# A chunked delta rule with routed experts: stacked keys in the front, block-diagonal copies by ScalarE, half blocks in 64x64 tiles, readerless products

## The chip, the core and the metric

The kernel runs on one core of a Trainium2 chip. Five engines run their own instruction streams: TensorE (PE, with its weight loads shown as PEld), VectorE (DVE), ScalarE (ACT), GpSimd (POOL) and SyncE (SP, which here only issues DMA transfers). They wait for each other by semaphores. The metric is the device time of one execution in microseconds. The profile comes from one execution of its own.

## The reference, cut to what matters

Two blocks follow each other. The first is a delta rule with B=4 batches, H=8 heads, 768 time steps and head size D=48; the second sends each of the 3072 resulting rows (384 wide) to one of eight experts.

```python
k_n = k / (np.linalg.norm(k, axis=-1, keepdims=True) + 1e-06)
state = np.zeros((B, H, D, D), dtype=np.float32)
for t in range(S):
    kt, vt, bt = (k_n[:, :, t], v[:, :, t], beta[:, :, t, None])
    y[:, :, t] = np.einsum('bhd,bhde->bhe', q[:, :, t], state)
    v_old = np.einsum('bhde,bhd->bhe', state, kt)
    state = state + bt[:, :, :, None] * np.einsum('bhd,bhe->bhde', kt, vt - v_old)
# ...  x = y as (3072, 384)
logits = x @ w_gate
expert_idx = np.argmax(logits, axis=1)
# ...  gate_w: the softmax of the chosen logit; rows sorted by expert
    h = np.maximum(x_sorted[lo:hi] @ w1[e], 0.0)
    y_sorted[lo:hi] = h @ w2[e]
# ...
return (gate_w[:, None] * y).astype(np.float32)
```

## The kernel before

Time is cut into 24 steps of C=32 tokens. The 128 partitions hold the 32 tokens of each of the four batches. For a step, PE forms the scores (keys by keys, keys by queries) of all heads; DVE masks them into `km`; DVE inverts the 32x32 triangular blocks of four steps (a group) at once, a long chain of small operations (`invert`). A step then takes the state's answer to its keys (`pv`, copied out as R), multiplies it by the inverted block (`pz`, copied out as Z), and adds keys by Z to the state (`acc`, copied out as `states`). Rows of the output go to DRAM (`xs`), their logits decide the expert, and after the last step the experts run over gathered rows.

Keys and queries lie in DRAM as `kq_t[step, 96, 4, 2, 128]`: two heads stacked on 96 partitions, four pairs, key or query, four batches of 32 tokens. A product over 96 partitions mixes the two heads of a pair, unless one operand is block-diagonal: `wide_kq` holds, for each of the two heads, a copy that is zero in the other's rows.

The program does not leave the order to a scheduler: instructions stand on each engine in the order in which these lines run.

How keys are loaded and scores formed:

```python
    def load_plain(c, k):

        t = kq_buffer()[0:D].rearrange("d p k t -> d (p k) t")
        for e, eng in enumerate((nc.sync, nc.scalar)):
            eng.dma_start(out=t[:, NP * e : NP * e + NP, :], in_=kq_t[c, D * e : D * e + D, :, k, :])
        return t

    def load_kq(c):
        if c < NS:
            if c not in kqs:
                kqs[c] = kq_buffer()
            nc.sync.dma_start(out=kqs[c][:], in_=kq_t[c])

    def load_wide(c):
        if c < NS:
            for e in range(2):
                r = slice(D * e, D * e + D)
                nc.sync.dma_start(out=wide_kq[c % 3][r, e], in_=kq_t[c, r])

    def plain_scores(pa, keys, others):

        for h in range(H):
            for b in range(B):
                j = NP * (h % 2) + h // 2
                nc.tensor.matmul(
                    pa[rows_of(b), C * h : C * h + C], lhsT=keys[:, j, rows_of(b)],
                    rhs=others[:, j, rows_of(b)], start=True, stop=True, skip_group_check=True,
                )

    def front_scores(c, pa):

        wide = wide_kq[c % 3]
        for p in range(NP):
            for b in range(B):
                for e in range(2):
                    nc.tensor.matmul(
                        pa[rows_of(b), 128 * p + 64 * e : 128 * p + 64 * e + 64],
                        lhsT=wide[:, e, p, 0, rows_of(b)], rhs=wide[:, e, p, :, rows_of(b)],
                        start=True, stop=True, skip_group_check=True,
                    )
        load_wide(c + 3)
        return c, pa

    def scores(c):

        if c >= NS:
            return None
        wide, kq = wide_kq[c % 3], kqs[c]
        pa = psA.tile([128, 512], FP32, name="pa", tag="pa")
        for p in range(NP):
            for b in range(B):
                nc.tensor.matmul(
                    pa[rows_of(b), 128 * p : 128 * p + 128], lhsT=kq[:, p, 0, rows_of(b)],
                    rhs=wide[:, :, p, :, rows_of(b)], start=True, stop=True,
                    skip_group_check=True,
                )
        load_wide(c + 3)
        return pa
```

The first group of steps (0 to 3) is inverted in halves of 16 tokens; two products by half blocks (`across`) then complete each of its steps. Copies by ACT with `own` as scale lay a block into two columns, one of them zero, so that two batches share a 64x64 tile:

```python
    def across(gt, fdt, ub, s):

        W = C // 2
        part = ub[:, H * s : H * s + H, W:C]
        m1 = work.tile([128, H, W], FP32, name="m1")

        def product(l, r):
            po = psA.tile([128, 512], FP32, name="pa", tag="pa")
            for h in range(H):
                for b in range(B):
                    nc.tensor.matmul(
                        po[rows_of(b), W * h : W * h + W], lhsT=l[rows_of(b), H * s + h],
                        rhs=r[rows_of(b), h], start=True, stop=True, skip_group_check=True,
                    )
            return po[:, 0 : H * W]

        po = product(gt, part)
        nc.scalar.activation(out=m1[:].rearrange("p h w -> p (h w)"), in_=po, func=AF.Copy)

        def second():
            po = product(fdt, m1)
            chores.appendleft(partial(added, po))

        def added(po):
            nc.vector.tensor_tensor(
                out=part, in0=part, in1=po.rearrange("p (h w) -> p h w", h=H), op=OP.add
            )

        chores.appendleft(second)

    def chore():
        if chores:
            chores.popleft()()

    def spread_out(steps=(0, GS)):

        g, ub = spread[0]
        if g not in ubs:
            ubs[g] = block.tile([128, GS * H, 2, C], FP32, name="ubw")
        a, b = (H * s for s in steps)
        for k in range(2):
            nc.scalar.activation(
                out=ubs[g][:, a:b, k], in_=ub[:, a:b], func=AF.Copy, scale=own[:, k : k + 1]
            )
        if steps[1] == GS:
            spread.popleft()
```

Products of the identity with itself, which nothing reads, keep TensorE at work, and `fill` gives DVE a budget of inversion work:

```python
    def heat(n=1, out=None):

        if out is None:
            out = psA.tile([128, 512], FP32, name="pa", tag="pa")[:]
        for _ in range(n):
            nc.tensor.matmul(
                out, lhsT=ident[:],
                rhs=ident[:].unsqueeze(1).to_broadcast([128, out.shape[1] // 128, 128]),
                start=True, stop=True, skip_group_check=True,
            )
```

A step, and the front and the loop around it:

```python
        if c == 0:
            R = vs
        else:
            by_state(pv, 0, False)
            R = work.tile([128, H, D], FP32, name="R")
            nc.scalar.activation(
                out=R[:].rearrange("q h w -> q (h w)"), in_=pv[:, 0:DM], func=AF.Copy
            )
            if c < LATE:
                ranked()
                logits()
        if c >= LATE:
            turn(c - 1)
        scale_v(c + 1, 0)
        for h in range(H):
            for r in two_of:
                nc.tensor.matmul(
                    pz[r, D * h : D * h + D],
                    lhsT=ub[r, H * s + h].rearrange("q k w -> q (k w)"),
                    rhs=R[r, h, :], start=(h == 0), stop=True, skip_group_check=True,
        chore()
        Z = work.tile([128, H, D], FP32, name="Z")
        # ... Z <- pz by ScalarE
        if c > 0:
            by_state(pq, 1, True)
        # ...
        load_kq(c + LEAD + 1)
        if c < GS:
            load_kq(c + GS)
        extra = score() if c in EXTRA else None
        scale_v(c + 1, 1)
        # ... acc += keys by Z; load_kt(c + 2); states <- acc; chore(); pq += km by Z
        nc.scalar.activation(out=x, in_=pq[:, 0:DM], func=AF.Copy, scale=-1.0)
        nc.sync.dma_start(out=xs[128 * c : 128 * c + 128, 0:DM], in_=x)
        if spread and GS <= c and c >= GS * (spread[0][0] - 1):
            spread_out()
        return extra

    # ... the front
    keys = [load_plain(c, 0) for c in range(GS)]
    nc.scalar.dma_start(out=cf[:, 0:CS], in_=src[:, 0:CS])
    nc.scalar.dma_start(out=beta[:], in_=beta_blk)
    for i in (1, 2, 0):
        t = wide_kq[i][:].rearrange("q e p k w -> q (e p k w)")
        for j, eng in enumerate(((nc.vector, nc.gpsimd), (nc.gpsimd, nc.vector))[i % 2]):
            eng.memset(t[:, 1024 * j : 1024 * j + 1024], 0.0)
    for c in range(GS, GS + 3):
        load_wide(c)
    queries = [load_plain(c, 1) for c in range(GS)]
    nc.gpsimd.memset(states[:], 0.0)
    nc.gpsimd.memset(empty[:], FAR)
    first = {c: ss for ss in BATCHES for c in ss}
    load_vt(0)
    load_kt(0)
    for c in range(1, LEAD + 1):
        kqs[c] = kq_buffer()
    load_kq(1)

    kms[0] = km_buffer()
    for c in range(GS):
        pool, name = ((psA, "pa"), (psQ, "pq"), (psC, "pv"), (psC, "pz"))[c]
        pa = pool.tile([128, 512], FP32, name=name, tag=name)
        plain_scores(pa, keys[c], keys[c])
        keep_plain(c, 0, pa[:, 0 : H * C], mask_0)
    behind.append([0, invert(0), 0.0])
    ahead = [front_scores(GS, acc[:, 2, :]), front_scores(GS + 1, acc[:, 3, :])]
    load_vt(1)
    load_kt(1)
    for c in range(GS):
        a = H * C * (c % 2)
        plain_scores(acc[:, c // 2, a : a + H * C], keys[c], queries[c])
    load_kq(2)
    ahead.append(front_scores(GS + 2, psC.tile([128, 512], FP32, name="pv", tag="pv")))
    load_kq(8)
    ahead.append(front_scores(GS + 3, psQ.tile([128, 512], FP32, name="pq", tag="pq")))
    load_kq(9)
    load_kq(3)
    heat(3)
    while not spread:
        fill(0.1)
    scale_v(0, 0)
    scale_v(0, 1)
    begin(0)
    chore()
    keep_plain(0, 1, acc[:, 0, :], mask[:, C : 2 * C])
    keep_scores(*ahead[0])
    chore()
    keep_scores(*ahead[1])
    chore()
    spread_out((0, 1))
    # ...
    for c in range(NS):
        # ...
        if c % GS == 0 and c // GS not in ubs:
            while not spread:
                fill(0.1)
            spread_out()
        extra = step(c)
        fill(4.0)
        # ...
        if c < GS - 1:
            chore()
            spread_out((c + 1, c + 2))
        # ...
        more = score()
        if c + 1 < NS:
            begin(c + 1)
        fill(3.2)
        keep_scores(*more)
        if c == GS:
            weights[0] = start_w(wpool)
            pieces.extend(pieces_w(moe_w1[0], moe_w2[0], *weights[0]))
        if pieces:
            pieces.popleft()()
```

Of the kernel before, what the change touches and what calls it, by code (L numbers as in the profile page):

```python
# [22 lines left out]
DD = 2 * D  # L23
# [8 lines left out]
E = 8  # L32
# [21 lines left out]
def _f32_consts():  # L54

    p = np.arange(128)[:, None]
    j = np.arange(128)[None, :]
    rev = np.broadcast_to(E - np.arange(E), (128, E))
    base = np.broadcast_to(np.arange(E) * LIST, (128, E))
    more = np.arange(E)[:, None] * LIST + CAP + np.arange(MAXR)[None, :] * 128
    more = np.broadcast_to(more.reshape(1, -1), (128, E * MAXR))
    t, w = p % C, j[:, :C]
    kk = 1.0 * (t == w) - (t < w)
    own = 1.0 * (p // C % 2 == np.arange(2)[None, :])
    half = t // (C // 2) == w // (C // 2)  # L70
    k0 = 1.0 * (t == w) - ((t < w) & half) - (t // (C // 2) > w // (C // 2))
    kq = -1.0 * (t < w)
    mine = -1.0 * (p // D == np.arange(2)[None, :])
    return np.concatenate(
        [kk, kq, k0, own, mine, rev, base, more, p < j, np.ones((128, 128))], axis=1
    ).astype(np.float32)
# [3 lines left out]
def kernel(  # L80
# [23 lines left out]
    CS = 3 * C + 4  # L104
# [3 lines left out]
    def part(w):  # L108
# [4 lines left out]
    mask, mask_0, own, mine, rev, base, further, upper, ones = (  # L113
        part(w) for w in (2 * C, C, 2, 2, E, E, E * MAXR, 128, 128)
# [164 lines left out]
    scored, front, now = [0], [None], [0]  # L279
# [34 lines left out]
    def load_plain(c, k):  # L314

        t = kq_buffer()[0:D].rearrange("d p k t -> d (p k) t")
        for e, eng in enumerate((nc.sync, nc.scalar)):
            eng.dma_start(out=t[:, NP * e : NP * e + NP, :], in_=kq_t[c, D * e : D * e + D, :, k, :])
        return t
# [6 lines left out]

    def load_wide(c):
        if c < NS:
            for e in range(2):
                r = slice(D * e, D * e + D)  # L330
                nc.sync.dma_start(out=wide_kq[c % 3][r, e], in_=kq_t[c, r])
# [11 lines left out]
    def plain_scores(pa, keys, others):  # L343

        for h in range(H):
            for b in range(B):
                j = NP * (h % 2) + h // 2
                nc.tensor.matmul(
                    pa[rows_of(b), C * h : C * h + C], lhsT=keys[:, j, rows_of(b)],
                    rhs=others[:, j, rows_of(b)], start=True, stop=True, skip_group_check=True,  # L350
                )

    def front_scores(c, pa):

        wide = wide_kq[c % 3]
        for p in range(NP):
            for b in range(B):
                for e in range(2):
                    nc.tensor.matmul(
                        pa[rows_of(b), 128 * p + 64 * e : 128 * p + 64 * e + 64],  # L360
                        lhsT=wide[:, e, p, 0, rows_of(b)], rhs=wide[:, e, p, :, rows_of(b)],
                        start=True, stop=True, skip_group_check=True,
                    )
        load_wide(c + 3)
        return c, pa

    def scores(c):
# [3 lines left out]
        wide, kq = wide_kq[c % 3], kqs[c]  # L371
        pa = psA.tile([128, 512], FP32, name="pa", tag="pa")
# [7 lines left out]
        load_wide(c + 3)  # L380
# [136 lines left out]
    def across(gt, fdt, ub, s):  # L517
# [3 lines left out]
        m1 = work.tile([128, H, W], FP32, name="m1")  # L521

        def product(l, r):
            po = psA.tile([128, 512], FP32, name="pa", tag="pa")
            for h in range(H):
                for b in range(B):
                    nc.tensor.matmul(
                        po[rows_of(b), W * h : W * h + W], lhsT=l[rows_of(b), H * s + h],
                        rhs=r[rows_of(b), h], start=True, stop=True, skip_group_check=True,
                    )  # L530
            return po[:, 0 : H * W]

        po = product(gt, part)
        nc.scalar.activation(out=m1[:].rearrange("p h w -> p (h w)"), in_=po, func=AF.Copy)

        def second():
            po = product(fdt, m1)
# [13 lines left out]
    def spread_out(steps=(0, GS)):  # L551

        g, ub = spread[0]
        if g not in ubs:
            ubs[g] = block.tile([128, GS * H, 2, C], FP32, name="ubw")
        a, b = (H * s for s in steps)
        for k in range(2):
            nc.scalar.activation(
                out=ubs[g][:, a:b, k], in_=ub[:, a:b], func=AF.Copy, scale=own[:, k : k + 1]
            )  # L560
        if steps[1] == GS:
            spread.popleft()
# [38 lines left out]
    def step(c):  # L601
        g, s = divmod(c, GS)
        kq, ub, kt, vs, km = kqs.pop(c, None), ubs[g], kts.pop(c), vss.pop(c), kms[g]
# [13 lines left out]
        else:  # L617
# [5 lines left out]
            if c < LATE:  # L623
                ranked()
                logits()
        if c >= LATE:
# [15 lines left out]
        if c > 0:  # L642
            by_state(pq, 1, True)
        if c >= LATE:
# [3 lines left out]
        if c == NS - 1:  # L648
            ahead_of_time(1)
        load_kq(c + LEAD + 1)  # L650
        if c < GS:
            load_kq(c + GS)
        extra = score() if c in EXTRA else None
        scale_v(c + 1, 1)
        if c < NS - 1:
# [10 lines left out]
            for e in range(2):  # L666
                nc.scalar.activation(  # L667
                    out=states[:, :, :, e], func=AF.Copy, scale=mine[0:DD, e : e + 1],
# [15 lines left out]
        if c == ss[0]:  # L684
            n = len(ss)
            xgs[c] = work.tile([128, n, ROW], FP32, name=f"xg{n}", bufs=3 if n == 1 else 2)
# [4 lines left out]
        if spread and GS <= c and c >= GS * (spread[0][0] - 1):  # L691
            spread_out()
        return extra

    def score():
        c = scored[0]
        scored[0] += 1
        return c, scores(c)
# [133 lines left out]
    keys = [load_plain(c, 0) for c in range(GS)]  # L832
    nc.scalar.dma_start(out=cf[:, 0:CS], in_=src[:, 0:CS])
    nc.scalar.dma_start(out=beta[:], in_=beta_blk)
    for i in (1, 2, 0):
        t = wide_kq[i][:].rearrange("q e p k w -> q (e p k w)")
        for j, eng in enumerate(((nc.vector, nc.gpsimd), (nc.gpsimd, nc.vector))[i % 2]):
            eng.memset(t[:, 1024 * j : 1024 * j + 1024], 0.0)
    for c in range(GS, GS + 3):
        load_wide(c)  # L840
    queries = [load_plain(c, 1) for c in range(GS)]
# [3 lines left out]
    load_vt(0)  # L845
    load_kt(0)
    for c in range(1, LEAD + 1):
        kqs[c] = kq_buffer()
    load_kq(1)

    kms[0] = km_buffer()
    for c in range(GS):
        pool, name = ((psA, "pa"), (psQ, "pq"), (psC, "pv"), (psC, "pz"))[c]
        pa = pool.tile([128, 512], FP32, name=name, tag=name)
        plain_scores(pa, keys[c], keys[c])
        keep_plain(c, 0, pa[:, 0 : H * C], mask_0)
    behind.append([0, invert(0), 0.0])
    ahead = [front_scores(GS, acc[:, 2, :]), front_scores(GS + 1, acc[:, 3, :])]
    load_vt(1)
    load_kt(1)  # L860
    for c in range(GS):
        a = H * C * (c % 2)
        plain_scores(acc[:, c // 2, a : a + H * C], keys[c], queries[c])
    load_kq(2)
    ahead.append(front_scores(GS + 2, psC.tile([128, 512], FP32, name="pv", tag="pv")))
    load_kq(8)
    ahead.append(front_scores(GS + 3, psQ.tile([128, 512], FP32, name="pq", tag="pq")))
    load_kq(9)
    load_kq(3)
    heat(3)  # L870
# [5 lines left out]
    chore()  # L876
    keep_plain(0, 1, acc[:, 0, :], mask[:, C : 2 * C])
# [4 lines left out]
    spread_out((0, 1))  # L882
# [12 lines left out]
    for c in range(NS):  # L895
# [3 lines left out]
        if c % GS == 0 and c // GS not in ubs:  # L899
            while not spread:  # L900
                fill(0.1)
            spread_out()
        extra = step(c)
        fill(4.0)
        if extra:
            keep_scores(*extra)
        if c < GS - 1:
            chore()
            spread_out((c + 1, c + 2))
# [9 lines left out]
        fill(3.2)  # L919
        keep_scores(*more)  # L920
        if c == GS:
# [193 lines left out]
```

## Time and profile before

| what | value |
|---|---|
| time, three runs | 635.75 us median (631.23 to 637.58) |
| span of the profiled execution | 630.8 us |
| recurrence with its front / experts | 309.0 us / 321.8 us |
| PE busy | 560.4 us (89%), 7660 products |
| PEld busy | 371.1 us (59%), 7661 loads |
| DVE busy | 249.0 us (39%), 818 instructions |
| ACT busy | 184.2 us (29%), 474 instructions |
| POOL busy | 105.1 us (17%), 111 instructions |
| moved by DMA | 68.97 MB |

A busy share over the whole span says little here, since the two parts have different limits; the profile is read by stages. In a row of the timeline, the first number is the start and the second the time from the first instruction of the group to the end of its last, in microseconds; in brackets stands the idle time of the engine ahead of it and what ended it. "issue" means that nothing which the profile shows ended the wait. In a row of waits stand the engine and line that waited, what it waited for, the sum in microseconds, how many times, and the longest. The clock is the share of TensorE's full clock that was granted.

### The profile page before, as it was taken

How to read it: one execution, taken by the hardware profiler on the slowest of the kernel's cores; microseconds unless marked ns; L12 is line 12 of the kernel's file. 1: busy time of each engine (PE TensorE's matmuls, PEld its weight loads, DVE VectorE, ACT ScalarE, POOL GpSimd, SP SyncE). 2: the span in 40 equal slices, each digit the busy share in tenths (PEclk: the TensorE clock that was granted, in tenths of full speed). 3: DMA queues.
4: the chain of work that ended last, by engine and by line, in shares of the span. 5: the costliest groups of instructions: out<-in, count | busy, mean ns of one | idle time of the engine just before them, and what ended most of it. 6: DMA issues, size and time to landing. Idle time of an engine off the chain costs nothing. (4 is left out here: it accounts for less than half of the span.)

```text
span 630.8 us, 17552 instructions
## 1 busy us (share of the span) xinstructions
PE 560.4 (89%) x7660; PEld 371.1 (59%) x7661; DVE 249.0 (39%) x818; ACT 184.2 (29%) x474; POOL 105.1 (17%) x111
## 2 busy tenths in 40 slices
PE   4378888879889899788999999999999999999990
PEld 4356666767767677566867555555555555455550
DVE  4845567997999979311410201111011110201100
ACT  0214536565465665563201101011011110111100
POOL 3000000010110202121137004014140231401011
PEclk9997758897888987685799999999999999999996
DMA  9857535676584322221017634223343223400000
GB/s 167 171 129 211 130 106 133 187 157 176 155 156 116 92 80 64 40 66 40 14 28 278 223 111 146 86 74 131 124 151 103 83 94 125 150 8 32 1 23 14
DMA packets 41632, 68.97 MB, mean 109 GB/s; under 512 B 10758, under 2 KB 31670, under 8 KB 41552
## 3 DMA queue, kind: packets, MB, share of 16 engines
q1 hardware_dynamic: 34128, 57.05, 33.4%
q0 software_dynamic: 4640, 9.47, 4.7%
q10 hardware_dynamic: 2784, 1.29, 1.2%
q8 instruction: 61, 1.00, 0.7%
q14 instruction: 19, 0.16, 0.1%
HBM read 59.02 MB, written 10.35 MB: 110 GB/s over the span
## 5 line engine op out<-in xcount | busy, mean ns | idle before, releaser
L993 PE MATMUL phe<-xTe,w1t 128*128 128x448 f32 (+1 forms) x384 | 136.2, 515 | 0.0
L1009 PE MATMUL pye<-w2t,hT 128*128 128x384 f32 x352 | 114.8, 486 | 0.0
L993 PEld LDWEIGHTS phe<-xTe,w1t 128*128 128x128 f32 x384 | 71.0, 190 | 60.4 <-issue 58.5
L1009 PEld LDWEIGHTS pye<-w2t,hT 128*128 128x128 f32 x352 | 66.9, 190 | 47.1 <-issue 2.6
L809 POOL DMA_INDIRECT lists<-ids,ri x24 | 24.0, 1001 | 277.8 <-DVE tmp L492 142.5
L998 DVE TENSOR_SCALAR hT<-phe 128x448 f32<-128x448 f32 (+1 forms) x32 | 18.9, 592 | 116.4 <-PE phe L993 104.3
L497 DVE TENSOR_TENSOR ut<-ut,tmp 128x58 f32<-128x58 f32 (+9 forms) x164 | 53.1, 324 | 5.4
L492 DVE TENSOR_TENSOR tmp<-ut 128x58 f32<-128x58 f32 (+9 forms) x164 | 52.8, 322 | 5.2
L180 POOL DMA_INDIRECT out_dram<-y,rows x22 | 21.9, 997 | 183.4 <-ACT y L1018 154.1
L571 ACT ACTIVATE vs<-vt,normt 128x48 f32<-128x48 f32 x192 | 47.9, 325 | 1.8 <-issue 1.8
L1002 ACT ACTIVATE hT<-phe 128x448 f32<-128x448 f32 (+1 forms) x32 | 16.6, 517 | 105.7 <-PE phe L993 105.7
L667 ACT ACTIVATE states<-acc,cf 96x768 f32<-96x768 f32 x46 | 38.7, 891 | 21.8 <-PE acc L659 19.4
L1018 ACT ACTIVATE y<-pye,xin 128x384 f32<-128x384 f32 x15 | 8.7, 581 | 122.5 <-PE pye L1009 122.5
L631 PE MATMUL pz<-R,ubw 64*64 64x48 f32 x736 | 29.9, 237 | 14.5 <-ACT lg L733 8.0
L988 DVE COPY xTe<-px 128x448 f32<-128x448 f32 (+1 forms) x24 | 13.3, 580 | 66.5 <-PE px L984 55.9
L631 PEld LDWEIGHTS pz<-R,ubw 64*64 64x64 f32 x736 | 26.8, 151 | 18.0 <-ACT lg L733 9.2
L678 PE MATMUL pq<-Z,km 32*32 32x48 f32 x1536 | 31.7, 230 | 6.3 <-issue 6.1
L678 PEld LDWEIGHTS pq<-Z,km 32*32 32x32 f32 x1536 | 25.5, 125 | 13.0 <-issue 12.6
L659 PE MATMUL acc<-Z,kt 32*96 32x96 f32 x736 | 29.1, 311 | 2.8 <-issue 1.5
L1014 DVE TENSOR_SCALAR y<-pye,xin 128x384 f32<-128x384 f32 x7 | 4.3, 618 | 68.3 <-PE pye L1009 68.3
L609 PEld LDWEIGHTS pv<-states,kq 96*32 96x32 f32 x736 | 17.4, 121 | 18.8 <-issue 11.7
L659 PEld LDWEIGHTS acc<-Z,kt 32*96 32x96 f32 x736 | 24.4, 210 | 6.4 <-issue 3.6
(142 smaller groups left out, 641.3 us busy)
## 6 DMA issues: line engine op xcount, KB each, us to landing
w1t<-in_moe_w_dram SPq DMA_DIRECT2D x7, 1536.0 KB, 12.3
w2t<-in_moe_w_dram SPq DMA_DIRECT2D x7, 1536.0 KB
kq<-in_kq_t_dram SPq DMA_DIRECT2D x23, 384.0 KB, 6.2
wkq<-in_kq_t_dram SPq DMA_DIRECT2D x40, 192.0 KB, 4.0
vt<-in_v_tok_dram SPq DMA_DIRECT2D x24, 192.0 KB, 2.9
kt<-in_k_tok_dram SPq DMA_DIRECT2D x24, 192.0 KB, 4.3
xs<-xg SPq DMA_DIRECT2D x24, 192.0 KB, 7.1
w1t<-in_moe_w_dram SPq DMA_DIRECT2D x6, 256.0 KB
```

Of the source, the lines that this page charges most:

```text
L180: nc.gpsimd.indirect_dma_start(out=out, out_offset=bass.IndirectOffsetOnAxis(ap=index, axis=0), in_=y[0:w, :], in_offset=None, bounds_chec ...
L492: nc.vector.tensor_tensor(out=tv, in0=ud[:, :, j + 1 : W, j].unsqueeze(3).to_broadcast([128, K, n, j]), in1=ud[:, :, j, 0:j].unsqueeze(2). ...
L497: nc.vector.tensor_tensor(out=ud[:, :, j + 1 : W, 0:j], in0=ud[:, :, j + 1 : W, 0:j], in1=tv, op=OP.add)
L571: nc.scalar.activation(out=vss[c][:, h, :], in_=vts[c][:, h, :], func=AF.Copy, scale=norms[g][:, H * s + h : H * s + h + 1],)
L631: nc.tensor.matmul(pz[r, D * h : D * h + D], lhsT=ub[r, H * s + h].rearrange("q k w -> q (k w)"), rhs=R[r, h, :], start=(h == 0), stop=Tru ...
L659: nc.tensor.matmul(acc[0:DD, b, DD * p : DD * p + DD], lhsT=kt[rows_of(b), 2 * p : 2 * p + 2, :], rhs=Z[rows_of(b), 2 * p : 2 * p + 2, :], ...
L667: nc.scalar.activation(out=states[:, :, :, e], func=AF.Copy, scale=mine[0:DD, e : e + 1], in_=acc[0:DD, :, 0:DM].rearrange("q b (p e w) -> ...
L678: nc.tensor.matmul(pq[rows_of(b), D * h : D * h + D], lhsT=km[rows_of(b), H * s + h, 1], rhs=Z[rows_of(b), h, :], start=(c == 0 and h == 0 ...
L809: nc.gpsimd.indirect_dma_start(out=lists, out_offset=bass.IndirectOffsetOnAxis(ap=ri[:, i : i + 1], axis=0), in_=ids[:, ss[i] : ss[i] + 1] ...
L993: nc.tensor.matmul(ph[:], lhsT=w1t[:, s, f * 128 : f * 128 + 128], rhs=xT[:, s, :], start=(s == 0), stop=(s == NK - 1),)
L998: nc.vector.tensor_scalar(out=hT[:, f, :], in0=ph[:], scalar1=0.0, scalar2=None, op0=OP.max)
L1009: nc.tensor.matmul(py[:], lhsT=hT[:, f, t * 128 : t * 128 + w], rhs=w2t[:, f, :], start=(f == 0), stop=(f == NF - 1),)
```

## The change

Four things are changed, and the instructions' order with them.

- **Stacked keys.** Steps 0 to 3 no longer load the 48 rows of each head by themselves and multiply head by head; they load stacked halves (keys first, queries later) and use a block-diagonal copy, so that one product serves a pair of heads.
- **Block-diagonal copies by ScalarE up to step 7.** The copies for steps 0 to 7 are made on the chip from the stacked tile, by an activation with a 0/1 scale per partition (four of them by DVE), and not loaded by two DMA transfers each into zeroed tiles. For later steps they are loaded as before, and those of steps 8 to 10 follow the front's other loads.
- **Half blocks in 64x64 tiles.** The products of `across` take two batches at once, with block-diagonal copies of the left factor, made by ScalarE for step 0 and by GpSimd for steps 1 to 3.
- **Readerless products.** A 128x256 product into `pz` precedes the block product of steps 1 to 15; some of 128x512 stand in the front, in step 0 and, once no scores are left to form, at the end of each step.

Besides, the blocks are spread step by step and not group by group, DVE's budget is 8.6 us and not 7.2 per step up to step 9, and the first expert's weights begin to load at step 9 and not 4.

```diff
-    def load_plain(c, k):
-        t = kq_buffer()[0:D].rearrange("d p k t -> d (p k) t")
-        for e, eng in enumerate((nc.sync, nc.scalar)):
-            eng.dma_start(out=t[:, NP * e : NP * e + NP, :], in_=kq_t[c, D * e : D * e + D, :, k, :])
-        return t
+    def load_half(c, k, eng):
+        if c not in kqs:
+            kqs[c] = kq_buffer()
+        eng.dma_start(out=kqs[c][:, :, k, :], in_=kq_t[c, :, :, k, :])
...
+    def widen(c):
+        for e in range(2):
+            nc.scalar.activation(
+                out=wide_of(c)[:, e], in_=kqs[c][:], func=AF.Copy, scale=this[0:DD, e : e + 1]
+            )
...
+    def widen_half(c, k, w, i):
+        for e in range(2):
+            out, in_ = w[:, e, :, i, :], kqs[c][:, :, k, :]
+            if e or k:
+                nc.scalar.activation(out=out, in_=in_, func=AF.Copy, scale=this[0:DD, e : e + 1])
+            else:
+                nc.vector.tensor_scalar(
+                    out=out, in0=in_, scalar1=this[0:DD, 0:1], scalar2=None, op0=OP.mult
+                )
...
+    def half_scores(c, pa, w, i):
+        for p in range(NP):
+            for b in range(B):
+                nc.tensor.matmul(
+                    pa[rows_of(b), 64 * p : 64 * p + 64], lhsT=kqs[c][:, p, 0, rows_of(b)],
+                    rhs=w[:, :, p, i, rows_of(b)], start=True, stop=True, skip_group_check=True,
+                )
...  # across
+        l1, l2 = (both(t[:, H * s : H * s + H], pool=s > 0) for t in (gt, fdt))
-                for b in range(B):
+                for q in two_of:
                     nc.tensor.matmul(
-                        po[rows_of(b), W * h : W * h + W], lhsT=l[rows_of(b), H * s + h],
-                        rhs=r[rows_of(b), h], start=True, stop=True, skip_group_check=True,
+                        po[q, W * h : W * h + W], lhsT=l[q, h].rearrange("q k w -> q (k w)"),
+                        rhs=r[q, h], start=True, stop=True, skip_group_check=True,
                     )
...  # step
             if c < LATE:
                 ranked()
                 logits()
+                heat(1, pz[:, 0:256])
...
+        else:
+            heat(1, pq[:])
...
-        if c < GS:
-            load_kq(c + GS)
...
-        if spread and GS <= c and c >= GS * (spread[0][0] - 1):
-            spread_out()
+        if c >= GS - 1:
+            spread_out(c + 1)
...  # score
+        if c >= NS:
+            heat()
...  # the front
+    for c in range(GS):
+        load_half(c, 0, (nc.sync, nc.scalar)[c % 2])
...
+    for c in range(GS, 2 * GS):
+        load_kq(c)
+    load_vt(0)
+    load_kt(0)
+    for c in range(GS):
+        load_half(c, 1, nc.sync)
+    for c in range(2 * GS, LEAD + 1):
+        load_kq(c)
+        load_vt(c - 2 * GS + 1)
+        load_kt(c - 2 * GS + 1)
...
+    for c in range(FRONT, FRONT + 3):
+        load_wide(c)
-    heat(3)
+    heat(4)
...
     chore()
+    heat(1, front[0][1][:])
...
     chore()
-    spread_out((0, 1))
+    heat(1, front[0][1][:])
+    spread_out(0)
...  # the loop
-        fill(4.0)
+        fill(4.0 if c > LEAD else 4.6)
...
-        fill(3.2)
+        fill(3.2 if c > LEAD else 4.0)
...
-        if c == GS:
+        if c == LEAD:
             weights[0] = start_w(wpool)
```

## The prediction

> **What bounds the kernel now.** I read the forty slices first: the first 309 us hold the recurrence and the last 321 us the experts, where PE is at 9 tenths and the granted clock at full rate. The change touches nothing in the second part, so I take its 321 us as fixed. I then cut the first part at the starts of the 24 evictions of `pz` (the ACT rows for Z, one per step; Z0 at 46.56, Z4 at 101.46, Z20 at 261.98 us) and asked for the busy time in each stage. The columns are PE, PEld, DVE, ACT, POOL, clock, DMA share, GB/s.
>
> ```profile
> 0.00:46.56 46.56, 25.03 (x998) 20.02 (x999) 26.71 (x77) 5.47 (x18) 5.81 (x13) 0.99 0.78 156
> 46.56:59.45 12.89, 10.91 (x340) 8.58 (x343) 9.26 (x38) 5.91 (x17) 0.00 (x0) 0.62 0.88 246
> 73.83:89.79 15.96, 12.16 (x299) 9.25 (x295) 9.70 (x30) 6.28 (x18) 0.00 (x0) 0.70 0.36 104
> 121.28:132.16 10.88, 9.53 (x240) 7.50 (x244) 9.85 (x37) 5.39 (x15) 2.10 (x2) 0.85 0.36 93
> 230.11:238.04 7.93, 7.27 (x219) 5.78 (x215) 7.11 (x32) 5.64 (x19) 0.97 (x1) 1.00 0.29 79
> 282.26:296.16 13.90, 12.04 (x211) 8.95 (x212) 1.87 (x14) 5.00 (x14) 3.69 (x4) 0.60 0.16 46
> ```
>
> Four regimes show. The front (46.56 us) has no engine busy for even 60% of it. Steps 0 to 3 last 54.9 us at a mean clock near 0.7. Steps 4 to 19 last 160.5 us with DVE busy for 134.2 us, the sum of those stages: DVE, which inverts the blocks, is the bound there. The last steps have an idle DVE and a step of 7.9 us at clock 1.00 but 13.9 us at 0.60.
>
> For the front I read the weight loads in order of time and who waited.
>
> ```profile
> 11.80 0.55 PEld L348 LDWEIGHTS pz<-kq 48*32 48x32 f32 x33 [2.24 <-issue]
> 12.41 2.89 PEld L359 LDWEIGHTS acc<-wkq 96*32 96x32 f32 x93
> 18.30 1.14 PEld L359 LDWEIGHTS acc<-wkq 96*32 96x32 f32 x35 [3.00 <-issue]
> 19.61 1.36 PEld L348 LDWEIGHTS acc<-kq 48*32 48x32 f32 x93 [0.17 <-issue]
> 24.77 1.80 PEld L348 LDWEIGHTS acc<-kq 48*32 48x32 f32 x128 [3.80 <-issue]
> 30.97 0.61 PEld L348 LDWEIGHTS acc<-kq 48*32 48x32 f32 x35 [4.40 <-issue]
> ```
>
> The loads between two "issue" waits are 33+93, 35+93 and 128: always about 128, each with a product beside it, so 256 instructions. The page's queues give the cause:
>
> ```profile
> q8 instruction: 61, 1.00, 0.7%
> ```
>
> 61 packets of 16.4 KB carry about 15,300 PE instructions, one packet per 256. PE is waiting for its own program, 13.4 us in these four waits, while data fill the DMA engines. What this delays is in the timeline:
>
> ```profile
> 30.00 1.02 DVE L509 STREAM_TRANSPOSE fdt<-ut 128x512 f32<-128x512 f32 x1
> 36.08 4.39 PE L584 MATMUL pa<-ident 128*128 128x512 f32 x6
> 40.53 0.73 PE L527 MATMUL pa<-ub,km 32*32 32x16 f32 x64
> ```
>
> DVE has the first inverse at 31.0; the product that reads it starts at 40.53, as PE still had scores and three readerless products in front of it.
>
> For the steps I read the waits, of DVE over 44 to 102 us and of PE over 102 to 222 us:
>
> ```profile
> DVE ub L541 <- PE pa L527: 10.9, 3, 5.0
> DVE km L399 <- PE pa L375: 6.9, 4, 4.4
> ```
> ```profile
> PE pz L631 <- ACT lg L733: 5.3, 11, 1.6
> ```
>
> In steps 0 to 3 DVE, which will be the bound later, loses 17.8 us waiting for PE: whatever makes PE earlier there hands DVE an earlier start on all its inversions. The third line is the gap that the new 128x256 product meets.
>
> [...] the same 32 score loads and products take 1.94 us at 52.10 and 1.08 us at 126.81. [...] 32 products in 64x64 tiles (57.37) take 1.14 us but 64 in 32x32 tiles (58.43) take 0.73 us: halving the count of half-block products saves program, not array time.
>
> **The change, part by part.**
>
> *Front program.* By the order of instructions the matmuls up to step 1's opening one fall from 595 to 343. Each is four instructions here (16 matmuls show as 32 loads and 32 products), so 252*4/256 = 3.9 blocks less: three of the four long waits should go. The stacked-key product of a step takes 32 records instead of 64.
>
> *Front data.* Keys for steps 0 to 3 (0.79 MB), whole kq for 4 to 7 (1.57), v and k of step 0 (0.39), queries (0.79), constants (0.15) must land before PE ends the front: 3.7 MB. Before moved 6.97 MB in 45 us at a mean 155 GB/s, about 190 while busy, so the last query lands near 22 us.
>
> *ScalarE copies.* 128x1024 takes 1.1 us (two in 2.19 us), 128x256 0.45 and 96x768 0.85. Eight 96x1024 copies at 1.1 and twelve 96x512 ones at about 0.6 (four more go to DVE) make 16 us, in step with the landings and done near 24. PE then has about 25 us, and heat(4), 8 records at 4.39/6 = 0.73 us, ends at 31. DVE's chain took 18.0 us from the last masked key (12.95); the memsets go, the stacked keys need a copy first, so it starts near 12 and ends near 30. The block product starts at 31 to 34 instead of 40.5: **-8 us**. The two readerless products after it fill waits of 0.4 and 1.3 us with about 1.6 us: +0.5.
>
> *Steps 0 to 3.* 31 matmuls less in each of steps 1 and 2: half a block each, -1 us with the 1.1 to 2.4 us per "issue" wait found there. Array time of six 64x64 half-block products +0.4 each, +2. The wide keys of step 8 are now queued behind a load that waits for step 0's state product, so step 0's scores wait some 2 us. Spreading one step (0.9 us) instead of four (2.19) ahead of step 4: -1.3. Better clock from the readerless products: PE is busy for 44.5 us at about 0.72; at 0.85 it is 38, -6. Sum: **-4 us**.
>
> *Steps 4 to 19.* The 128x256 product waits, in the order of instructions, for ACT's lg, and so does the block product: R is already there. So it doesn't fill that wait but follows it, 2 records at some 0.2 us at full clock, +0.4 us on PE's chain in each of 14 steps. DVE is the bound there, so most of that hides. Its larger budget up to step 9 (8.6 us instead of 7.2 per step) and fewer half-clock stages let DVE go from 84% to perhaps 87%: 134.2/0.87 = 154, **-6 us**.
>
> *Steps 20 to the end of the recurrence.* 47 us at clocks 0.60, 1.00, 0.60, 0.50. Steps at 1.00 take 8.7. A 128x512 product per step from step 15 costs up to 0.85 us where nothing else waits, and if it keeps half the slow stages warm: **-4 us** net.
>
> Sum: -8 + 0.5 - 4 - 6 - 4 = -21.5 us, 635.75 to **614 us**.
>
> **The rivals.** (1) *Data, not program, holds the front.* [...] if the queries land near 30 rather than 22, the front gains 3 us instead of 8. The DMA share of 0.9 over the first 28 us speaks for it, the 3 MB less to move before the product against. It gives 619 us. (2) *The readerless product is pure cost.* If the clock doesn't change, 14*0.4 and 9*0.6 add 11 us and the clock gains (6 + 4 + some of 6) go: 628 us. For it: it stands behind lg, in no wait of its own. Against: stages at full clock are 2 to 6 us shorter than the slow ones. (3) *The clock stays full throughout.* Steps 20 to 24 at 8.7 to 10 us and DVE at 92% give another 12 us: 602 us.
>
> **Range and chances.** Rival 3 sets the low end, 602; between rivals 1 and 2 lies the high end, 626. A gain of over 2% means under 623.0 us; only rival 2, or rival 1 with half of the clock gain gone, misses that. Faster 0.78, within 2% 0.19, slower 0.03.
>
> **What would show it.** Right: "issue" waits of under 4 us in sum ahead of the first block product; that product at 31 to 34 us; Z4 near 90, Z20 near 245; about 56 packets on the instruction queue; clock of the stages after Z4 nearer to 0.95. Wrong: PE waiting for DMA or ACT's copies past 28 us in the front; step 0's scores waiting over 3 us for the wide keys; the wait of the block product for lg replaced by the readerless product with clocks still at 0.6 to 0.8; experts of other than 321 us.

## The result, and the profile after

The changed kernel takes 615.55 us in the median of four runs (606.83 to 620.98), against 636.66 us of the kernel before on the same chip. The ratio is 0.9588, with a 95% interval of 0.9464 to 0.9712: faster.

The profile comes from an execution of 617.1 us, a slow one for this kernel. A second profile of the same kernel (run e5, below) has 608.6 us; where the two differ, both are given. First the queue that carries PE's program, from the page's list of queues (packets, MB, share):

```profile
q8 instruction: 56, 0.92, 0.7%
```

Five packets less, as counted. Next the stages between the Z evictions, with the same columns as before (PE, PEld, DVE, ACT, POOL busy; clock; DMA share; GB/s):

```profile
0.00:41.13 41.13, 27.49 (x525) 20.02 (x527) 27.24 (x86) 23.15 (x43) 8.79 (x17) 0.92 0.53 134
41.13:60.04 18.91, 16.50 (x274) 12.20 (x277) 10.19 (x36) 5.90 (x17) 3.75 (x5) 0.50 0.61 158
74.43:84.17 9.74, 9.29 (x271) 7.25 (x266) 7.27 (x25) 6.28 (x18) 0.00 (x0) 1.00 0.51 145
121.77:132.43 10.66, 9.51 (x241) 7.32 (x242) 10.03 (x34) 6.17 (x17) 2.02 (x2) 0.91 0.65 141
220.30:230.75 10.45, 8.18 (x215) 6.14 (x211) 9.28 (x36) 6.33 (x20) 0.97 (x1) 1.00 0.50 105
271.10:282.46 11.36, 9.54 (x215) 7.26 (x215) 1.87 (x14) 5.67 (x16) 3.69 (x4) 0.85 0.36 87
```

The front has half the records of before on PE (525 for 998) and four times the work on ACT. Step 2 (third row) fell from 15.96 to 9.74 us at full clock; step 0 (second row) grew from 12.89 to 18.91 at half clock. Rows 4 and 5 belong to the stretch that the prediction has bound by DVE. Row 4 is step 7, which took 10.44 us in the kernel before (the prediction's row at 121.28 us is step 6). Row 5 is step 17 both times and takes 10.45 us for 7.93 at the same full clock, with DVE busy for 9.28 us and not 7.11.

The sums by stretch, where an expert's first `phe` product ends the last one:

| stretch | before | after | after again (e5) |
|---|---|---|---|
| front, to Z0 | 46.6 us | 41.1 us | 38.3 us |
| steps 0 to 3, Z0 to Z4 | 54.9 us | 51.6 us | 44.4 us |
| steps 4 to 19, Z4 to Z20 | 160.5 us | 159.9 us | 161.3 us |
| Z20 to the first expert product | 68.4 us | 63.8 us | 64.1 us |
| from there to the end | 300.4 us | 300.7 us | 300.5 us |

PE's weight loads in the front show what took the place of the waits for program:

```profile
8.33 0.87 PEld L368 LDWEIGHTS pv<-wkq,kq 96*32 96x32 f32 x32 [1.19 <-issue]
13.04 0.84 PEld L368 LDWEIGHTS pz<-wkq,kq 96*32 96x32 f32 x32 [3.85 <-ACT wkq L348]
15.12 1.48 PEld L382 LDWEIGHTS acc<-wkq,kq 96*32 96x32 f32 x32 [1.24 <-ACT wkq L329]
17.20 1.48 PEld L382 LDWEIGHTS acc<-wkq,kq 96*32 96x32 f32 x32 [0.60 <-ACT wkq L329]
26.26 0.49 PEld L368 LDWEIGHTS acc<-wkq,kq 96*32 96x32 f32 x32 [0.73 <-ACT wkq L348]
```

Of the four long "issue" waits of before one of 1.19 us is left; PE now waits for ScalarE's copies, 0.6 to 1.2 us a time, and once 3.85 us for the keys of step 3. The first block product starts at 32.01 us where it was 40.53.

### The profile page after: what moved, and what is told of

Read it like the earlier page. It is cut to its first block, busy times and chain, and to the rows that moved or that the text cites. A ratio compares the mean times of both kernels' runs of the same rounds, so it can differ in the third digit from the quotient of the medians.

```text
span 617.1 us, 16442 instructions
## 1 busy us (share of the span) xinstructions
PE 568.3 (92%) x7076; PEld 370.3 (60%) x7077; DVE 248.4 (40%) x820; ACT 207.1 (34%) x529; POOL 113.3 (18%) x120
## 5 line engine op out<-in xcount | busy, mean ns | idle before, releaser
L1041 DVE TENSOR_SCALAR hT<-phe 128x448 f32<-128x448 f32 (+1 forms) x32 | 18.9, 591 | 116.4 <-PE phe L1036 96.2
L692 ACT ACTIVATE states<-acc,cf 96x768 f32<-96x768 f32 x46 | 38.7, 891 | 16.4 <-PE acc L684 15.3
L1031 DVE COPY xTe<-px 128x448 f32<-128x448 f32 (+1 forms) x24 | 13.3, 580 | 66.5 <-PE px L1027 55.9
L656 PE MATMUL pz<-R,ubw 64*64 64x48 f32 x736 | 28.5, 231 | 4.5 <-ACT R L644 4.1
L703 PE MATMUL pq<-Z,km 32*32 32x48 f32 x1536 | 27.7, 228 | 2.7 <-issue 2.7
L684 PE MATMUL acc<-Z,kt 32*96 32x96 f32 x736 | 27.6, 294 | 1.0 <-issue 1.0
L703 PEld LDWEIGHTS pq<-Z,km 32*32 32x32 f32 x1536 | 23.5, 124 | 7.1 <-issue 6.7
L684 PEld LDWEIGHTS acc<-Z,kt 32*96 32x96 f32 x736 | 22.9, 195 | 5.6 <-issue 2.1
L203 POOL DMA_INDIRECT xin<-xs,rows x22 | 22.4, 1019 | 10.7 <-DMA rowh<-lists 4.6
```

The lines of the kernel that those rows point to most:

```text
L203: nc.gpsimd.indirect_dma_start(out=xin[0:w, t, :], out_offset=None, in_=xs, in_offset=bass.IndirectOffsetOnAxis(ap=index, axis=0), bounds_ ...
L656: nc.tensor.matmul(pz[r, D * h : D * h + D], lhsT=ub[r, H * s + h].rearrange("q k w -> q (k w)"), rhs=R[r, h, :], start=(h == 0), stop=Tru ...
L684: nc.tensor.matmul(acc[0:DD, b, DD * p : DD * p + DD], lhsT=kt[rows_of(b), 2 * p : 2 * p + 2, :], rhs=Z[rows_of(b), 2 * p : 2 * p + 2, :], ...
L692: nc.scalar.activation(out=states[:, :, :, e], func=AF.Copy, scale=minus[0:DD, e : e + 1], in_=acc[0:DD, :, 0:DM].rearrange("q b (p e w) - ...
L703: nc.tensor.matmul(pq[rows_of(b), D * h : D * h + D], lhsT=km[rows_of(b), H * s + h, 1], rhs=Z[rows_of(b), h, :], start=(c == 0 and h == 0 ...
```

## The experiments

Each run below is timed against the kernel before on the same chip, in three series on three chips (e1 to e4, e5 to e8, e9 to e12; the changed kernel itself ran only in the second); ratios carry their 95% interval. A stage time comes from the one profile of its run, and the clock scatters from profile to profile (Z0 to Z1 of the changed kernel: 0.50 and 0.78), so differences of stages under some 2 us are not read.

**e5: the changed kernel again.** No edit.

> The changed kernel once more, as the reference for the others of this series on the same chip. Both theories expect a ratio to before of 0.955 to 0.970. If the 18.9 us from Z0 to Z1 in its first profile came from the wait for the wide keys of step 8 alone, they come again; if half of it was the phase in which the clock fell, this profile shows 14 to 16 us as the three other variants with the same front did, and the wait for the wide keys (2.4 us) again.

612.04 us in the median against 633.8 (602.67 to 623.15, too scattered for an interval). Z0 to Z1 was 15.3 us, with a 3.9 us wait of the scores for the wide keys. So about 3.5 us of the 18.9 came with the half clock that the first profile has from 34.9 us on, before Z0. That didn't come again, and what set it off isn't shown; the wait for the keys came again.

**e1: no early v and k of step 2.**

```diff
         load_kq(c)
-        load_vt(c - 2 * GS + 1)
-        load_kt(c - 2 * GS + 1)
+        if c == 2 * GS:
+            load_vt(1)
+            load_kt(1)
```

> The front no longer loads v and k of step 2; nothing else is changed. Theory (the wide keys of step 8 were queued behind a load that waits for step 0's state product, so step 0's scores waited 2.4 us for them [...]): the start of the score product of step 0 comes within 0.5 us of the end of the output products before it, Z0 to Z1 falls from 18.9 us to 14 to 16, ratio to before 0.945 to 0.955. Rival (step 0 is slow because the clock is at half rate anyway from 35 us on[...]): the wait goes but Z0 to Z1 stays over 17.5 us, ratio 0.957 to 0.962.

606.62 us against 631.96, ratio 0.9624 (0.9549 to 0.9699). In PE's timeline of the changed kernel, step 0's scores stand behind a wait (named after DVE, which had long been done; what they wait for is the landing of `wkq`, which SyncE issued at 44.9 us, after the `kt` load that needed step 0's `acc`):

```profile
46.21 1.50 PE L703 MATMUL pq<-Z,km 32*32 32x48 f32 x64
50.12 1.93 PE L382 MATMUL pa<-wkq,kq 96*32 96x128 f32 x32 [2.41 <-DVE tmp L500]
```

In e1 they follow at once and at full clock, and the step takes half of what it took:

```profile
40.73 1.01 PE L703 MATMUL pq<-Z,km 32*32 32x48 f32 x64
41.67 1.08 PE L382 MATMUL pa<-wkq,kq 96*32 96x128 f32 x32
```
```profile
38.06:47.53 9.47, 9.45 (x278) 7.11 (x281) 8.54 (x35) 5.90 (x17) 3.74 (x5) 1.00 0.39 112
```

Z0 to Z1 is 9.5 us here, in e6 and in e9, which all lack the early loads; e2, e3, e4, e5, e10 and e11, which have them, show 14.8 to 15.6 at clocks of 0.77 and 0.78, and the first profile 18.9. The theory holds for the wait, and its size was too small: 5 to 6 us, since a lower clock went with the wait (the scores behind it take 1.94 us in e2 and e5, 1.08 in e1). The ratio is another matter: 0.9624 lies in the rival's range and not in the theory's. Z4 comes at 76.7 us (80.4 to 85.8 in e2, e3 and e4 on the same chip), but Z20 at 242.5 (241.0 to 246.3 there): what step 0 gained is gone by then.

**e2: the fourth step's keys first.**

```diff
-        load_half(c, 0, (nc.sync, nc.scalar)[c % 2])
+        load_half(c, 0, nc.scalar if c == 1 else nc.sync)
```

> The fourth step's keys are issued on SyncE's queue ahead of the whole tiles of steps 4 to 7, and not on ScalarE's beside them. Theory (in the changed kernel DVE's chain began at 14.6 us and not at 12 because these keys shared the DMA engines with later data and landed at 12.3): the last masked keys are done by 11.5 us, the chain ends 3 us earlier, and the first block product follows it by as much only if PE's program and readerless products are done by then: 29 to 30 us and not 32.0; ratio 0.950 to 0.955. Rival (ScalarE's 16 us of copies and the data behind them hold PE): the chain ends earlier but the block product stays at 31.5 or later, ratio 0.957 to 0.961.

609.98 us against 631.96, ratio 0.9649 (0.9516 to 0.9782): no gain over the changed kernel can be told by time. By profile the mechanism is there. DVE's last masked keys and the first transposition of its chain, in the changed kernel and in e2:

```profile
14.19 0.42 DVE L396 TENSOR_TENSOR km<-pz,cf 128x256 f32<-128x256 f32 x1 [1.11 <-PE pz L368]
14.65 2.17 DVE L429 STREAM_TRANSPOSE ut<-km 128x256 f32<-128x256 f32 x4
```
```profile
9.83 0.42 DVE L396 TENSOR_TENSOR km<-pz,cf 128x256 f32<-128x256 f32 x1 [0.43 <-PE pz L368]
10.29 2.15 DVE L429 STREAM_TRANSPOSE ut<-km 128x256 f32<-128x256 f32 x4
```

The chain starts 4.4 us earlier and the block product at 28.7 us instead of 32.0, now right behind the readerless products, which end at 28.6. Z4 comes at 80.4 us, but Z20 at 246.3.

**e6: both changes of order.** The edits of e1 and e2 together.

> Both changes of order: step 2's v and k no longer loaded in the front, the fourth step's keys ahead of later data. If the two gains add: first block product at 27 to 29 us, Z0 near 34, Z1 near 44, Z4 near 73, and a ratio 0.01 below the changed kernel's of the same series. Rival (DVE's inversions bound everything up to step 20, so what the front gives is taken back): Z4 as early, but Z20 still at 241 to 246 us as in the four variants so far, and the ratio within 0.005 of the changed kernel's.

605.69 us against 633.8, ratio 0.9572 (0.9528 to 0.9615). The block product came at 30.7 us, behind the four readerless products of the front, which ended at 30.6; Z1 at 46.9, Z4 at 75.8 us and not 73. Z20 came at 234.1 us. It is earlier than in the other profiles, so the rival's fixed Z20 falls, but Z4 to Z20 is 158.3 us, as ever. Against the changed kernel's median of the same series the gain is 1%, and the scatter of that kernel's runs is larger.

**e3: no 128x256 products.**

```diff
                 ranked()
                 logits()
-                heat(1, pz[:, 0:256])
```

> The 128x256 product ahead of the block product in steps 1 to 15 is left out. Theory of the prediction (it costs 0.4 to 0.6 us a step on PE, mostly hidden behind DVE, and buys clock): the mean clock from Z1 to Z15 falls by 0.05 or more, and the time from Z1 to Z15 grows by 2 to 5 us; ratio 0.962 to 0.968. Rival (pure cost): the clock stays within 0.03 and Z1 to Z15 shrinks by 5 to 8 us; ratio 0.946 to 0.951. Third (DVE hides cost and gain alike): within 2 us either way.

610.29 us against 631.96, ratio 0.9724 (0.9632 to 0.9815). Mixed: the clock from Z1 to Z15 stayed (0.92, with the products 0.92 and 0.94), Z1 to Z15 shrank to 136.0 us from 143.2 and 140.0, but the time did not. No theory holds whole; e9 takes it up.

**e4: no late 128x512 products.**

```diff
         scored[0] += 1
-        if c >= NS:
-            heat()
         return c, scores(c)
```

> The 128x512 product at the end of steps 15 to 23 is left out. Theory (it keeps the clock up where PE has no scores to form, and that is worth more than its 0.85 us): the mean clock from Z16 to the end of the recurrence falls from about 0.89 to 0.75 or less and this stretch grows by 3 to 6 us; ratio 0.963 to 0.968. Rival (pure cost): the clock stays within 0.03, the stretch shrinks by 4 to 6 us; ratio 0.949 to 0.953.

610.31 us against 631.96, ratio 0.9668 (0.9574 to 0.9761). The clock from Z16 to the first expert product fell to 0.82 (0.87 and 0.85 with them), and the stretch took 103.4 us (104.8 and 105.4 with them). Both theories miss, each by its other half: the clock fell, but no change of time that could be read came of it. Within the stretch, Z20 to the first expert product is 66.4 us, longer than in any other profile of the changed kernel and its variants (55.9 to 64.1), and Z16 to Z20 is shorter (37.0 us, with the products 41.0 and 41.3).

**e7: the readerless products alone, in the kernel before.**

```diff
                 logits()
+                heat(1, pz[:, 0:256])
...
         scored[0] += 1
+        if c >= NS:
+            heat()
```

> The kernel before, with the 128x256 product ahead of the block product in steps 1 to 15 and the 128x512 one at the end of steps 15 to 23, and nothing else of the change. Theory of the prediction (they bring 5 to 8 us by the clock): mean clock from Z1 to Z15 over 0.88 (0.84 without), ratio 0.985 to 0.992. Rival (they cost what they bring, and the whole gain is the front's and the first steps'): ratio 0.995 to 1.01, Z1 to Z15 within 3 us of 153.

638.42 us against 633.8, ratio 1.0071 (1.0007 to 1.0135). The theory's 0.985 to 0.992 is excluded: by themselves these products bring the old kernel nothing, and cost it 0.7%, just clear of noise. Its one profile has a clock of 0.80 from Z1 to Z15, and not over 0.88; Z1 to Z15 takes 163.6 us there, so the rival's 153 misses too. The products of the front and of step 0 are not in this run, and no run leaves them out of the changed kernel.

**e8: half blocks back in 32x32 tiles.** Also without the block-diagonal copies.

```diff
-        l1, l2 = (both(t[:, H * s : H * s + H], pool=s > 0) for t in (gt, fdt))
+        l1, l2 = (t[:, H * s : H * s + H] for t in (gt, fdt))
...
-                for q in two_of:
+                for b in range(B):
                     nc.tensor.matmul(
-                        po[q, W * h : W * h + W], lhsT=l[q, h].rearrange("q k w -> q (k w)"),
-                        rhs=r[q, h], start=True, stop=True, skip_group_check=True,
+                        po[rows_of(b), W * h : W * h + W], lhsT=l[rows_of(b), h],
+                        rhs=r[rows_of(b), h], start=True, stop=True, skip_group_check=True,
```

> The changed kernel with the half-block products back in 32x32 tiles, 32 of 0.73 us in all and not 16 of 1.0 to 1.9 us, without the block-diagonal copies of ScalarE and GpSimd. Theory of the prediction (the 64x64 form saves half a block of program per step and costs as much array time): Z0 to Z3 within 1.5 us of the changed kernel's of this series, ratio within 0.004. Rival (fewer instructions matter, as in the front): Z0 to Z3 longer by 3 us or more and an issue wait of over 1 us in each of the steps 0 to 2.

616.87 us against 633.8, ratio 0.9702 (0.963 to 0.9773). Z0 to Z3 is 43.6 us, with 64x64 tiles 35.8 (e5): the rival holds, but for step 0, whose wait for program is 0.7 us and not over 1. By time alone, with e5's runs so scattered, the 0.8% between the medians would not show it. PE's waits in e8 from Z0 to Z4 (longest three), and then its timeline in step 2:

```profile
PE pq L703 <- issue: 4.5, 3, 2.1
PE pa L382 <- DVE tmp L500: 2.2, 1, 2.2
PE acc L684 <- issue: 1.8, 2, 1.1
```
```profile
58.61 1.08 PE L382 MATMUL pa<-wkq,kq 96*32 96x128 f32 x32
...
71.24 0.52 PE L703 MATMUL pq<-Z,km 32*32 32x48 f32 x11 [2.14 <-issue]
71.69 1.94 PE L382 MATMUL pa<-wkq,kq 96*32 96x128 f32 x32
73.56 1.65 PE L619 MATMUL pv<-vs,ident 128*128 128x384 f32 x2
```

The waits for program are 6.3 us (e5: 0.3). After the last of them the same scores take 1.94 us and not 1.08, and most of the rest of the step runs at that pace too: step 2 takes 16.4 us, in e5 9.9. That the wait brought the clock down is not shown: the scores at 58.61 run at full pace behind a wait of 1.6 us, and e12 has a slow step 2 with no such wait.

**e12: half blocks in 64x64 tiles alone, in the kernel before.** The same edit of `across` the other way round, with the copies.

> The kernel before with the half-block products in 64x64 tiles and nothing else of the change. New theory (steps 0 to 3 ran at the pace at which PE's program comes in: 180 matmuls a step are 2.8 blocks of 256 instructions[...]): Z0 to Z4 falls from 54.9 us to 45 to 49, issue waits there from 6.5 us to under 2.5, ratio 0.982 to 0.990. Rival, the prediction's sizing (half a block saved, as much array time added): Z0 to Z4 53 to 56 us, ratio 0.996 to 1.002.

619.79 us against 627.8, ratio 0.9883 (0.9813 to 0.9954). Z0 to Z4 fell from 54.9 to 46.2 us. PE's waits for "issue" in that stretch before:

```profile
PE pa L375 <- issue: 2.4, 1, 2.4
PE pq L678 <- issue: 1.5, 2, 0.8
PE acc L659 <- issue: 1.5, 1, 1.5
PE pa L527 <- issue: 1.1, 1, 1.1
```

All of PE's waits of that stretch, in e12:

```profile
PE pz L646 <- ACT lg L751: 2.6, 3, 2.0
PE acc L674 <- ACT Z L653: 0.8, 1, 0.8
PE pz L646 <- ACT R L635: 0.6, 1, 0.6
PE pa L528 <- issue: 0.4, 1, 0.4
```

"issue" went from 6.5 us in five waits to 0.4. The new theory holds in every number that it gave, and 6.1 of the 8.7 us are the waits themselves. What sets the clock is not shown. Step 2 of e12:

```profile
70.12:83.27 13.15, 12.88 (x272) 10.47 (x268) 8.79 (x25) 6.28 (x18) 0.00 (x0) 0.63 0.47 129
```

It ran at clock 0.63 with PE busy for 12.88 of 13.15 us, and no wait in the 10 us ahead of it was over 0.5 us.

**e11: DVE's old budget.**

```diff
-        fill(4.0 if c > LEAD else 4.6)
+        fill(4.0)
...
-        fill(3.2 if c > LEAD else 4.0)
+        fill(3.2)
```

> The changed kernel with DVE's budget of 7.2 us per step throughout, as before. Theory of the prediction (the larger budget up to step 9 fills DVE better): Z4 comes later by 1 to 4 us, since the inverse that step 4 needs is not done in time, Z4 to Z20 stays at 158 to 164 us, ratio 0.966 to 0.972. Rival (PE waits for DVE's larger portions): Z0 to Z4 shorter and the ratio under 0.960.

609.24 us against 627.8, ratio 0.9725 (0.9624 to 0.9825). Z0 to Z4 is 45.8 us against 44.4 in e5, with step 3 at 10.2 us, where the seven profiles with the larger budget and the same products have 8.5 to 8.7, and a PE wait of 2.1 us in it where e5 has 0.3; Z4 to Z20 161.1. So by profile the larger budget is worth some 1.5 us ahead of step 4 and nothing later; by time alone, with no run of the changed kernel on that chip, it isn't settled.

**e10: spreading by group.** `spread_out(c + 1)` per step replaced for steps 4 to 23 by the old rule and two copies of a whole group.

```diff
-        if c >= GS - 1:
-            spread_out(c + 1)
+        if spread and GS <= c and c >= GS * (spread[0][0] - 1):
+            spread_group()
```

> The changed kernel with the blocks of steps 4 to 23 spread group by group as before (two copies of 1.1 us), not step by step (two of 0.45). Theory (the 1.3 us saved at each group whose inverse comes late is what shortened the last steps, since the 128x512 products don't): Z20 to the first expert's products grows from 59 to 64 us to 66 to 69, ratio 0.970 to 0.976 against 0.962 to 0.967 of the changed kernel. Rival (the last steps are shorter for the clock alone): within 2 us, same ratio.

607.07 us against 627.8, ratio 0.973 (0.9665 to 0.9795). Z20 to the first expert product took 58.8 us and not the 66 to 69 of the theory. It falls: how blocks are spread isn't what shortened the last stretch. The ratio lies in the theory's range, but with no run of the changed kernel on that chip it decides nothing.

**e9: both changes of order, and no 128x256 products.** The edits of e1, e2 and e3 together.

> Both changes of order in the front, and no 128x256 products: what the runs so far suggest as the better kernel. Theory (DVE's inversions bound steps 4 to 19, so neither the clock that the 128x256 product brings nor its 0.4 us a step reaches the end): Z4 at 74 to 76 us, Z4 to Z20 156 to 164 us, ratio within 0.004 of the 0.957 with both changes of order alone. Rival (the product is cost where PE ends a step): ratio 0.948 to 0.952.

590.1 us against 627.8, ratio 0.9415 (0.9358 to 0.9472): better than both kernels, and than e6's 0.9528 to 0.9615 on another chip. The rival's direction holds, by more than it said. A stage at full clock shows the cost of the product, first step 3 of e1, with it, then of e9, without:

```profile
67.99:76.68 8.69, 8.42 (x243) 6.43 (x244) 7.26 (x19) 6.18 (x17) 0.00 (x0) 1.00 0.62 164
```
```profile
69.59:77.37 7.78, 7.51 (x241) 6.00 (x243) 4.88 (x12) 6.17 (x17) 0.00 (x0) 1.00 0.61 172
```

0.9 us a step where PE has no slack. In the profiled execution of e9 (594.4 us) the clock from Z1 to Z15 was 0.81, and step 2 took 13.6 us at clock 0.60. That the product would have prevented this is not shown: e3, without it too, has 10.0 us at clock 1.00 there. Where in the recurrence the 1.6% of time went can't be read from that one profile, and in e3, with the same product left out but the old order of loads, no gain was seen: that they need each other is a guess.

## Why the prediction was right, point by point

The sum was right, 614 us for 615.55, but two of its terms were wrong in opposite directions, so that it came so close is in part luck. Of the signs that it named, "issue" waits under 4 us ahead of the block product (1.0), that product at 31 to 34 us and 56 packets came; so did one sign of being wrong, a wait of over 3 us for the wide keys (3.9 in e5).

- **Front, -8 us.** Right: -8.3 in e5, -5.4 in the first profile, with the product at 31.5 and 32.0 us as told. That one "issue" wait of 1.2 us is left, and 56 packets, confirms the count of blocks. The front moves less data as well, and no run changes its program alone, so how much of the 8 us is program and how much is data is not separated. What ended last was not PE behind its readerless products, as in the working, but DVE's chain: it started at 14.65 us and not near 12, because the fourth keys landed at 12.3 us behind later data. This is the first rival in part, for the keys and not for the queries, whose copies follow on ScalarE without a gap from 21.2 us; e2 shows it.
- **Wide keys of step 8, +2 us.** The mechanism was right and the size was not: 2.4 and 3.9 us of wait, but 5 to 6 us of step, as e1 shows; by Z20 it was gone.
- **Half blocks, a wash.** Wrong. The step that failed is "half a block each, -1 us with the 1.1 to 2.4 us per 'issue' wait", set against "+2" of array time. The array time is as told (32 records in 1.11 us at full clock). But some 180 matmuls a step kept PE at the pace of its program, 149 don't: nearly all the waits went, 6.0 us of them between e8 and e5, 6.1 between the kernel before and e12. e12 measures the whole at -8.7 us, and the two profiles e8 and e5 differ by 8.9 from Z0 to Z4. The rest beyond the waits is shorter work on PE at a better clock (busy 44.5 us before, 42.0 in e12), and what sets that clock stays open: in e8 the scores behind a wait of 2.14 us take 1.94 us and those behind one of 1.64 us take 1.08, and in e12 step 2 had a clock of 0.63 with no wait over 0.5 us ahead of it.
- **Clock by readerless products, -6 us in steps 0 to 3.** Wrong in its cause. The better clock came (0.92 from Z0 to Z4 in e5, 0.72 before), but e3 has 0.92 without the 128x256 products, and e7, with them, has 0.69. e12, with no new readerless product at all, has 0.79. Whether those of the front and of step 0 make up the difference is untested.
- **Steps 4 to 19, -6 us.** Wrong: nothing. Z4 to Z20 lies between 155 and 166 us in all fourteen profiles but e7's (173.1), at clocks from 0.83 to 0.93 and with Z4 from 75.8 to 101.5 us. DVE is busy for 134.6 us there after, 134.2 before: 84% both times, where the prediction had 87%. That DVE bounds it agrees with this, though not with the 10 us by which the stretch differs between runs of equal DVE work; no run changed DVE's work itself, so it is argued and not shown.
- **The 128x256 product, +0.4 us a step.** It does follow ACT's lg, as told from the order of instructions. The changed kernel's timeline of PE ahead of Z12:

```profile
173.00 0.70 PE L608 MATMUL pz<-ident 128*128 128x256 f32 x2 [0.27 <-ACT lg L763]
173.63 1.13 PE L656 MATMUL pz<-R,ubw 64*64 64x48 f32 x32
```

  The block product starts 0.63 us later for it, and 0.9 us a step are lost in the end. For the second rival, pure cost, e7 and e9 speak on this product, while e3 shows no gain from leaving it out; on the kernel it was wrong.
- **The end, -4 us.** The size was right (-4.6, -4.3), its cause wasn't: from Z16 on the 128x512 products bring nothing that could be read, and behind Z20 the time is only 2.3 to 2.6 us longer without them (e4); the spreading isn't it either (e10). e12 has 60.5 us there against 68.4 with neither, e7 68.4 with these products. The cause stays open. Over the fourteen profiles the stretch tends to be shorter where its clock is better, from 68.4 us at 0.76 before to 55.9 us at 0.97 in e9, so what differs between one profile of each may be mostly the clock. (The step of 7.9 us that the prediction put among the last steps is step 17, where DVE is busy; the one at full clock behind Z20 takes 8.7.)

So steps 0 to 3 brought 10.5 us in e5 and not 4, steps 4 to 19 brought 0 and not 6, and the two errors nearly cancelled. In the first profile, with its half clock ahead of step 2, steps 0 to 3 brought only 3.3 us.

## What to carry to other kernels

Where an engine with thousands of tiny instructions shows "issue" waits at even distances in its count of instructions (here 256), count the program: halving the number of half-block products took 8.7 us off Z0 to Z4 here (e12), although 32 records in 64x64 tiles took 1.11 us (e5) where 64 in 32x32 tiles had taken 0.73. Products that nothing reads should prove their worth by themselves (here 1.0071 in e7), and belong only into waits that really are waits: look up, in the order of instructions, which semaphore they stand behind. And a load moved ahead must not stand, on its queue, behind one that waits for a buffer of a later step (2.4 us of wait in the first profile of the changed kernel, 3.9 in e5, none in e1).

## What the runs showed of the hardware

- PE's packets of 256 instructions came no closer than about 3.5 us apart in the steps of the kernel before, and 6.4 us in the first 28 us of its front (8.66, 15.05, 21.80, 28.24 us by the trace), where the DMA share was 0.99; PE resumed 1.3 to 1.7 us after the end of the packet that it waited for.
- In the changed kernel two transfers issued on ScalarE's queue from 1.2 to 2.6 us shared the engines with 1.6 MB issued on SyncE's from 2.2 to 4.3 us; the second landed only at 12.3 us. Issued on SyncE's queue ahead of those data, its keys were masked by 10.3 us (e2).
- A copy of 96x512 by a 0/1 scale took DVE 0.48 us and ScalarE 0.71, or 4.99 us for eight in a row; two of 128x256 took GpSimd 1.8 to 2.0 us and ScalarE 0.9 (changed kernel).
